# Two tokens of V in a partition row, heads in pairs on halves of the matmul array: one change to an attention and routed-expert kernel

## The chip, the cores and the metric

The kernel runs on one core of one Trainium2 chip. The metric is the device time of one execution in microseconds; the time of the kernel before is the median of three runs, and one further execution was profiled.

## The reference

Attention of 8 batches x 8 heads with head dimension 64: 512 local tokens that attend to a band of 32 tokens on each side and to 32 global tokens, and 32 global tokens that attend to everything. Its output, 8 x 544 rows of 512 numbers, goes through eight experts with a capacity of 80 rows each; a row that no expert keeps comes out as zeros.

```python
s_g = scale * q_g @ k_all.T                    # global queries over all keys
out_g = softmax(s_g) @ v_all
s_ll = where(abs(i - j) <= 32, scale * q_l @ k_l.T, -1e9)
s_lg = scale * q_l @ k_g.T
out_l = softmax(concat(s_lg, s_ll)) @ concat(v_g, v_l)
x = concat(out_g, out_l)                       # (4352, 512)
probs = softmax(x @ w_gate); expert = argmax; gate = its probability
for e in range(8):
    rows = those of e, cut to the 80 of the largest gate
    out[rows] = gate[rows] * (relu(x[rows] @ w1[e]) @ w2[e])
```

## The kernel before

The program is written out in order by hand: what stands first in the source stands first on its engine. A step q is half a batch, four heads; there are 16 steps, and the loop over them (L691 to L819) interleaves the work of steps q to q + 4. An index t or u below counts blocks of 64 or 128 tokens of a head, j = 0, 1 a pair of heads.

- SP issues nearly all loads: `load_qk` (q and k four steps ahead), `load_v` (V two steps ahead, L214, and with every even step the global values vg of the batch, four transfers, L218, into one of two buffers). After them in a step come the stores of x (`Ld`) and some stores of zeros to the output (`zeros`, L638): 17 in all, six in the loop and eleven behind it.
- V lies in `vb` with one token of a head in a partition: 128 partitions, 16 blocks of 64 numbers and a 1 beside them that makes the sum of the weights. The rows that a transfer moves are 256 bytes. `shift_v` (POOL, L224 to L226) makes a second copy shifted by 64 tokens, for the odd blocks.
- `T_chunk` transposes q and k on PE (L299); ACT copies them to SBUF (L307). `kO_copy` and `qw_copy` (POOL) make the wrapped ends and the shifted copy of k.
- `L_fill(q, j)` puts the banded scores of two heads into two PSUM tiles, 16 matmuls of 64 rows by 128 columns (L362), one head on the upper and one on the lower half of the rows; the band of the first head is added by a matmul with `bandneg` (L353), that of the second is multiplied in by POOL after the exponential (`mask`, L375).
- `G_fill` and `Q_fill` make the scores against global keys (L328) and of global queries (L340, five matmuls of 128 x 128 for each j).
- `G_all` (L396) begins the output of all four heads with the global part, `H_chunk(q, h)` (L409) adds the local part of one head: eight products, each as two passes of fp32, 128 rows by 64 columns. After heads 1 and 3, DVE divides by the sum (L416, L417) into `xn`. `Q_chunk` (L432) does the same for the global queries.
- `X_chunk` transposes `xn` for the gate's logits (L447), `C_chunk` (POOL, L458) packs it for the store; `La` to `Ld` make logits, gates and the stores of a batch, spread over the next steps; `some(n)` runs pieces of the list of the best rows on DVE. `warm(n)` are matmuls whose result nobody reads.

In a step the order on PE is: G_all, H(0), Q_chunk, T(q+2), L_fill(q+1, 0), H(1), L_fill(q+1, 1), T(q+2), H(2), H(3), G_fill(q+1), Q_fill, X, Q_fill, X. Expert weights come on POOL's queue, one or two parts of 512 KB a step. Behind the loop stand the choice of rows (DVE), the gathers (L912), the experts and the scatters (L950).

Of the kernel before, what the change touches and what calls it, by code (L numbers as in the profile page):

```python
# [26 lines left out]
def _np_consts(B, S, SG, cap):  # L27
# [5 lines left out]
    p = np.arange(P)[:, None]  # L33
    i = np.arange(64)[None, :]
    band = np.zeros((P, 8, 64), dtype=np.float32)
    for t in range(8):
        w = p if t % 2 == 0 else np.where(p < 64, p + 64, p - 64)
        band[:, t, :] = (w - i >= 0) & (w - i <= 2 * WIN)
    band[:, 7, :] *= (p >= 64) == (i < 32)
# [43 lines left out]
def kernel(  # L83
# [57 lines left out]
    vb = [vpool.tile([P, 32, 65], FP32, name=f"vb{i}") for i in range(3)]  # L141
# [45 lines left out]
    band = cpool.tile([P, 8, 64], FP32, name="band")  # L187
# [12 lines left out]
    def preset_v(i):  # L200
        nc.vector.memset(vb[i][:, 0:16, 64:65], 1.0)
# [4 lines left out]
    vg = [apool.tile([P, 2, 65], FP32, name=f"vg{i}") for i in range(2)]  # L206
    for i in range(2):
        nc.gpsimd.memset(vg[i][:, :, 64:65], 1.0)

    def load_v(q):  # L210
        b, qd = divmod(q, 2)
        hs = slice(4 * qd, 4 * qd + 4)
        v = vb[q % 3]
        nc.sync.dma_start(out=v[:, 0:16, 0:64], in_=v_l[b, hs].rearrange("h (u p) d -> p (h u) d", p=P))  # L214
        if qd == 0:
            for r in range(4):
                h = 2 * (r % 2) + r // 2
                nc.sync.dma_start(out=vg[b % 2][32 * r:32 * r + 32, :, 0:64],  # L218
                                  in_=v_g[b].rearrange("(q f) g d -> f g q d", f=4)[h])

    def shift_v(q):

        v = vb[q % 3][:].rearrange("p (o h u) d -> p o h (u d)", o=2, u=4)
        nc.gpsimd.tensor_copy(out=v[0:64, 1, :, 0:195], in_=v[0:64, 0, :, 65:260])  # L224
        nc.gpsimd.tensor_copy(out=v[0:64, 1, :, 195:260], in_=v[0:64, 0, :, 0:65])
        nc.gpsimd.tensor_copy(out=v[64:128, 1], in_=v[64:128, 0])  # L226

    load_v(0)
    load_qk(1)
# [12 lines left out]
    def load_wg():  # L242
        nc.sync.dma_start(out=wg[:, :, 0:E], in_=moe_w_gate.rearrange("(c p) e -> p c e", p=P))
        for q in range(2):
            nc.sync.dma_start(out=wgq[64 * q:64 * q + 64],
                              in_=moe_w_gate[256 * q:256 * q + 256].rearrange("(h d) e -> d h e", d=64))
# [18 lines left out]
    def setup_globals(b0, b1, *ts):  # L265
        for t, bd in ((1, kbd), (0, qbd)):
# [9 lines left out]
            for x, y, r, f in parts:  # L276
                nc.vector.tensor_copy(out=bd[x, b0:b1, r, 32 * f:32 * f + 32], in_=src[y, :, :, f, :])


    qkT = [apool.tile([P, 2, 1120], FP16, name=f"qkT{i}") for i in range(2)]  # L280
    kO = [apool.tile([P, 2, 4, 2, 64], FP16, name=f"kO{i}") for i in range(2)]
# [14 lines left out]
    def T_chunk(q, t, cp=None):  # L296
        T_ps = psT([P, 8, 2, 64], FP16, f"T_ps{q}_{t}")
        for i in range(8):
            nc.tensor.transpose(out=T_ps[:, i].rearrange("x a p -> x (a p)"),  # L299
                                in_=qkr[q][:, t, i].rearrange("p g d -> p (g d)"), identity=ident16[:, :])  # L300
        dst = qkT[q % 2][:, :, 544 * t:544 * t + 512].rearrange("x a (p i) -> x a p i", i=8)
        src = T_ps[:].rearrange("x i a p -> x a p i")
        if cp:
            for a in range(2):
                cp[a](out=dst[:, a], in_=src[:, a])
        else:
            nc.scalar.copy(out=dst, in_=src)  # L307

    def qw_copy(q):

        (nc.gpsimd if q else nc.vector).tensor_copy(out=qkT[q % 2][:, :, 512:544], in_=qkT[q % 2][:, :, 0:32])

    def kO_copy(q, *aa):

        for a in aa or range(2):
            eng = nc.gpsimd if q or a else nc.vector
            buf = qkT[q % 2][:, a]
            eng.tensor_copy(out=buf[:, 1056:1120], in_=buf[:, 544:608])
            eng.tensor_copy(out=kO[q % 2][:, a],  # L319
                            in_=buf[:, 608:1120].rearrange("x (u w y) -> x u w y", w=2, y=64)[:, :, ::-1, :])  # L320

    def G_fill(q):
# [4 lines left out]
        for j in range(2):  # L327
            nc.tensor.matmul(out=g_ps[64 * j:64 * j + 64, :], lhsT=kbd[:, b, 2 * qd + j, :],  # L328
                             rhs=qkT[q % 2][:, j, 32:544], start=True, stop=True)
        nc.scalar.activation(out=s["eG"][:], in_=g_ps[:], func=AF.Exp, scale=scale)  # L330

    def Q_fill(q, j):
        b, qd = divmod(q, 2)
        gq_ps = psS([P, NB, 64], FP32, f"gq_ps{q}_{j}")
        for u in range(NB):
            if u < 4:
                k = qkT[q % 2][:, j, 544 + 128 * u:672 + 128 * u]
            else:
                k = kbd[:, b, 2 * qd:2 * qd + 2, :].rearrange("x r c -> x (r c)")
            nc.tensor.matmul(out=gq_ps[:, u, :], lhsT=k, rhs=qbd[:, b, 2 * qd + j, :], start=True, stop=True)  # L340
        eQ = hpool.tile([P, NB, 64], FP32, tag="eQ", bufs=4, name=f"eQ{q}_{j}")
        nc.scalar.activation(out=eQ[:], in_=gq_ps[:], func=AF.Exp, scale=scale)
        st[q]["eQ"].append(eQ)

    def L_fill(q, j):

        s = st.setdefault(q, {"eL": {}, "eQ": []})
        buf = qkT[q % 2][:, j]
        l_ps = [psS([P, 512], FP32, f"l_ps{q}_{j}_{hh}") for hh in range(2)]
        under = q >= QB  # L350
        if under:

            nc.tensor.matmul(out=l_ps[0][:], lhsT=ident16[:, :], rhs=bandneg[:].rearrange("p t i -> p (t i)"),  # L353
                             start=True, stop=False, skip_group_check=True)
        for t in range(8):
            for hh in range(2):
                o = 64 * hh
                if t % 2 == 0:
                    lhsT = buf[o:o + 64, 544 + 64 * t:672 + 64 * t]
                else:  # L360
                    lhsT = kO[q % 2][o:o + 64, j, t // 2].rearrange("x w y -> x (w y)")
                nc.tensor.matmul(out=l_ps[hh][:, 64 * t:64 * t + 64], lhsT=lhsT,  # L362
                                 rhs=buf[o:o + 64, 64 * t + 32:64 * t + 96], start=(hh == 1 or not under), stop=True,
                                 skip_group_check=True)
        for hh in range(2):
            eL = hpool.tile([P, 512], FP32, tag="eL", bufs=8, name=f"eL{q}_{j}_{hh}")
            nc.scalar.activation(out=eL[:], in_=l_ps[hh][:], func=AF.Exp, scale=scale)  # L367
            s["eL"][2 * hh + j] = eL

    def mask(q, j):  # L370

        for hh in range(q >= QB, 2):
            eng = nc.gpsimd if q else nc.vector
            eL = st[q]["eL"][2 * hh + j]
            eng.tensor_tensor(out=eL[:], in0=eL[:], in1=band[:].rearrange("p t i -> p (t i)"), op=ALU.mult)  # L375
# [11 lines left out]
    def G_all(q):  # L387
# [3 lines left out]
        s["o2"] = [psO(f"o_ps{q}_{i}")[:, :, 0:260].rearrange("p h (u d) -> p h u d", u=4) for i in range(2)]  # L391
        s["o"] = [s["o2"][h // 2][:, h % 2] for h in range(4)]
        for u in range(4):
            for r in range(4):
                h = 2 * (r % 2) + r // 2
                nc.tensor.matmul(out=s["o"][h][:, u, :],  # L396
                                 lhsT=s["eG"][32 * r:32 * r + 32, 128 * u:128 * u + 128],
                                 rhs=vg[b % 2][32 * r:32 * r + 32, qd, :], start=(u == 0), stop=False,
                                 skip_group_check=True)

    def H_chunk(q, h):
# [3 lines left out]
        o = s["o"][h]  # L405
        for u in range(4):
            for odd in range(2):
                t = 2 * u + odd
                nc.tensor.matmul(out=o[64 * odd:64 * odd + 64, u, :],  # L409
                                 lhsT=s["eL"][h][:, 64 * t:64 * t + 64],  # L410
                                 rhs=v[:, 16 * odd + 4 * h + u, :], start=False, stop=True,
                                 skip_group_check=True)
        if h % 2:
            o2 = s["o2"][h // 2]
            rec = hpool.tile([P, 2, 4], FP32, tag="rec", bufs=4, name="rec")
            nc.vector.reciprocal(out=rec[:], in_=o2[:, :, :, 64])  # L416
            nc.vector.tensor_tensor(  # L417
                out=s["xn"][:, :, 64 * h - 64:64 * h + 64].rearrange("p u (h d) -> p h u d", h=2),
                in0=o2[:, :, :, 0:64], in1=rec[:].unsqueeze(3).to_broadcast([P, 2, 4, 64]), op=ALU.mult)

    def Q_chunk(q):
# [3 lines left out]
        og = psT([P, 65], FP32, f"og{q}")  # L425
        for u in range(NB):
            for h in range(4):
                f = slice(32 * (h // 2), 32 * (h // 2) + 32)
                r = 2 * (h % 2) + h // 2
                x = slice(32 * r, 32 * r + 32)  # L430
                eQ = s["eQ"][h % 2]
# [568 lines left out]
```

## Time and profile before

| | us |
|---|---|
| runs | 272.04, 274.37, 275.7 (median 274.37) |
| profiled execution | 272.33 |
| its span, first to last instruction | 270.6 |
| mean granted clock of TensorE | 0.937 |
| start of the vg matmuls of steps 1, 8, 9, 14, 15 | 25.6, 102.4, 116.3, 168.2, 183.5 |
| start of the first gather | 226.65 |

The span falls into three parts: loads and the first step up to 25.6 us, the loop up to about 191 us, and the choice of rows, gathers and experts. In the page a row names line, engine, operation, result<-inputs, shapes and number, then busy time and mean of one in ns, then the idle time before it and what ended that. "issue" stands for idle time that ended with nothing the profile shows. Matmuls overlap in the array, so PE's busy time isn't the time that the array computes; the distance between starts is the better measure.

The costliest rows of PE and POOL:

```profile
L375 POOL TENSOR_TENSOR eL<-eL,band 128x512 f32<-128x512 f32 x30 | 38.6, 1285 | 21.9 <-ACT eL L367 21.7
...
L409 PE MATMUL o_ps<-vb,eL 128*64 128x65 f32 x1024 | 43.9, 231 | 0.4 <-issue 0.3
...
L224 POOL COPY vb<-vb 64x780 f32<-64x780 f32 x16 | 13.9, 868 | 7.6 <-DMA vb<-in_v_l_dram 7.6
...
L226 POOL COPY vb<-vb 64x1040 f32<-64x1040 f32 x16 | 17.0, 1064 | 0.9
```

### The profile page before, as it was taken

Reading aid. Unit: us, or ns where it says so; the run is one execution under the profiler, and the core shown is the slowest. Engines: PE = TensorE matmul, PEld = TensorE weight load, DVE = VectorE, ACT = ScalarE, POOL = GpSimd, SP = SyncE. Lnnn points to the kernel's source line nnn. Section 1 sums busy time; section 2 is a strip of 40 time slices with the busy share of each in tenths; the row PEclk is TensorE's granted clock in tenths of the full one; section 3 lists DMA queues with packets and bytes.
Section 4 is the critical chain, followed back from the end, with each engine's and each line's share of the span. In section 5 each row is a group of like instructions: output and inputs, shape, how many; then the busy total and the mean of one; then the engine's idle time right before and its main releaser. Section 6 shows DMA issues by size and latency. Waiting matters only on the chain.

```text
span 270.6 us, 9574 instructions
## 1 busy us (share of the span) xinstructions
PE 234.3 (87%) x4031; PEld 160.4 (59%) x4031; DVE 151.7 (56%) x447; ACT 134.7 (50%) x236; POOL 165.2 (61%) x260
## 2 busy tenths in 40 slices
PE   6888898999899958989999999979939999479990
PEld 2467666776686747667677676557414435357750
DVE  2657534636743763478477689286878972002210
ACT  4657569679569580859669668240130000023430
POOL 2539987698697808777887898674540004752231
PEclk9799999999999996899999999795997999959997
DMA  7999899977989699899999899998999999289811
GB/s 226 253 305 221 276 249 239 289 165 156 299 255 205 226 216 277 152 240 310 174 275 262 174 207 167 268 208 159 162 205 223 233 417 417 91 161 212 208 48 48
DMA packets 67739, 60.05 MB, mean 222 GB/s; under 512 B 46192, under 2 KB 50544, under 8 KB 67696
## 3 DMA queue, kind: packets, MB, share of 16 engines
q1 hardware_dynamic: 59712, 40.61, 52.3%
q0 software_dynamic: 7840, 18.80, 39.1%
q8 instruction: 31, 0.51, 0.8%
q14 instruction: 12, 0.10, 0.1%
q10 hardware_dynamic: 144, 0.03, 0.1%
HBM read 61.57 MB, written 14.70 MB: 282 GB/s over the span
## 4 chain that ended last, share of the span: by engine, by line
PE 40%; DMA 19%; issue 12%; POOL 10%; DVE 5%; SPq 5%; ACT 5%; POOLq 1%; ACTq 0%; DVEq 0%
PE o_ps L409 9%; DMA vg<-in_v_g_dram 6%; PE o_ps L396 5%; DMA x_scr<-xgb 5%; PE og L432 5%; PE T_ps L299 4%; PE x_ps L447 3%; PE lt_ps L472 3%; DMA x_scr<-xb 3%; PE l_ps L362 3%; ACT qkT L307 3%; POOL out_dram L950 2%; DMA out_dram<-zt 2%; SPq L218 2%; PE l_ps L353 2%
## 5 line engine op out<-in xcount | busy, mean ns | idle before, releaser
L375 POOL TENSOR_TENSOR eL<-eL,band 128x512 f32<-128x512 f32 x30 | 38.6, 1285 | 21.9 <-ACT eL L367 21.7
L307 ACT COPY qkT<-T_ps 128x1024 f16<-128x1024 f16 x31 | 31.5, 1017 | 36.1 <-PE T_ps L299 35.9
L409 PE MATMUL o_ps<-vb,eL 128*64 128x65 f32 x1024 | 43.9, 231 | 0.4 <-issue 0.3
L409 PEld LDWEIGHTS o_ps<-vb,eL 128*64 128x64 f32 x1024 | 35.7, 141 | 11.7 <-issue 7.7
L367 ACT ACTIVATE eL<-l_ps 128x512 f32<-128x512 f32 x64 | 35.1, 606 | 12.6 <-PE l_ps L362 12.5
L165 ACT CAST qkr<-qkb 128x1024 f16<-128x1024 f32 (+1 forms) x26 | 26.9, 1040 | 3.8 <-DMA qkb<-in_q_l_dram 3.5
L651 PE MATMUL w_ps<-w1sb,onesb 128*128 128x512 bf16 x121 | 28.7, 391 | 0.0
L936 ACT ACTIVATE fhT<-h_ps 128x320 bf16<-128x320 f32 x16 | 6.5, 431 | 40.9 <-remote 39.3
L912 POOL DMA_INDIRECT xg<-x_scr,idx x8 | 7.8, 974 | 28.7 <-DMA out_dram<-zt 26.5
L396 PE MATMUL o_ps<-vg,eG 32*128 32x65 f32 x512 | 20.8, 291 | 3.8 <-DMA vg<-in_v_g_dram 3.8
L447 PE MATMUL x_ps<-misc,xn 128*128 128x128 f32 x128 | 21.0, 288 | 3.4 <-DVE xn L417 2.6
L417 DVE TENSOR_TENSOR xn<-o_ps,rec 128x512 f32<-128x512 f32 x32 | 22.1, 692 | 2.5 <-DVE rec L416 0.5
L416 DVE RECIPROCAL rec<-o_ps 128x8 f32<-128x8 f32 x32 | 6.6, 206 | 29.9 <-PE o_ps L409 29.9
L396 PEld LDWEIGHTS o_ps<-vg,eG 32*128 32x128 f32 x512 | 18.3, 199 | 6.6 <-DMA vg<-in_v_g_dram 4.3
L299 PE MATMUL T_ps<-ident,qkr 128*128 128x128 f16 x256 | 20.3, 223 | 1.8 <-ACT qkr L165 1.2
L458 POOL CAST xb<-xn 128x1024 bf16<-128x1024 f32 x16 | 16.6, 1039 | 6.7 <-DVE xn L417 6.7
L651 PEld LDWEIGHTS <-onesb 128*128 128x128 bf16 x121 | 11.6, 100 | 14.9 <-issue 2.9
L319 POOL COPY kO<-qkT 128x512 f16<-128x512 f16 x31 | 19.0, 614 | 1.9
L224 POOL COPY vb<-vb 64x780 f32<-64x780 f32 x16 | 13.9, 868 | 7.6 <-DMA vb<-in_v_l_dram 7.6
L950 POOL DMA_INDIRECT out_dram<-y,idx x8 | 7.4, 928 | 17.9 <-ACT y L948 17.3
L299 PEld LDWEIGHTS <-qkr 128*128 128x128 f16 x256 | 15.2, 99 | 4.6 <-ACT qkr L165 1.9
L226 POOL COPY vb<-vb 64x1040 f32<-64x1040 f32 x16 | 17.0, 1064 | 0.9
(156 smaller groups left out, 474.0 us busy)
## 6 DMA issues: line engine op xcount, KB each, us to landing
out_dram<-zt SPq DMA_DIRECT2D x17, 512.0 KB, 7.0
qkb<-in_q_l_dram SPq DMA_DIRECT2D x16, 512.0 KB, 5.4
qkb<-in_k_l_dram SPq DMA_DIRECT2D x16, 512.0 KB, 6.7
vb<-in_v_l_dram SPq DMA_DIRECT2D x16, 512.0 KB, 9.1
w2sb<-in_moe_w_dram POOLq DMA_DIRECT2D x12, 512.0 KB
w1sb<-in_moe_w_dram POOLq DMA_DIRECT2D x10, 512.0 KB
x_scr<-xb SPq DMA_DIRECT2D x8, 385.5 KB, 9.7
vb<-in_moe_w_dram POOLq DMA_DIRECT2D x6, 512.0 KB
```

The lines of the kernel that those rows point to most:

```text
L165: cp(out=qkr[q][:, t, i].rearrange("p i g d -> p g i d"), in_=qkb[q % 2][:, t, :, i])
L226: nc.gpsimd.tensor_copy(out=v[64:128, 1], in_=v[64:128, 0])
L299: nc.tensor.transpose(out=T_ps[:, i].rearrange("x a p -> x (a p)"), in_=qkr[q][:, t, i].rearrange("p g d -> p (g d)"), identity=ident16[:, :])
L307: nc.scalar.copy(out=dst, in_=src)
L319: eng.tensor_copy(out=kO[q % 2][:, a], in_=buf[:, 608:1120].rearrange("x (u w y) -> x u w y", w=2, y=64)[:, :, ::-1, :])
L367: nc.scalar.activation(out=eL[:], in_=l_ps[hh][:], func=AF.Exp, scale=scale)
L375: eng.tensor_tensor(out=eL[:], in0=eL[:], in1=band[:].rearrange("p t i -> p (t i)"), op=ALU.mult)
L396: nc.tensor.matmul(out=s["o"][h][:, u, :], lhsT=s["eG"][32 * r:32 * r + 32, 128 * u:128 * u + 128], rhs=vg[b % 2][32 * r:32 * r + 32, qd, ...
L409: nc.tensor.matmul(out=o[64 * odd:64 * odd + 64, u, :], lhsT=s["eL"][h][:, 64 * t:64 * t + 64], rhs=v[:, 16 * odd + 4 * h + u, :], start=F ...
L417: nc.vector.tensor_tensor(out=s["xn"][:, :, 64 * h - 64:64 * h + 64].rearrange("p u (h d) -> p h u d", h=2), in0=o2[:, :, :, 0:64], in1=re ...
L447: nc.tensor.transpose(out=x_ps[:, 128 * u:128 * u + 128], in_=s["xn"][:, u, 128 * j:128 * j + 128], identity=identf[:, :])
L651: nc.tensor.matmul(out=w_ps[:], lhsT=onesb[:], rhs=w1sb[0][:, 0, 0:512], start=True, stop=True)
```

## The change

V is laid out with two neighbouring tokens of a head in a partition row: 64 partitions hold 128 tokens, heads 0 and 1 of a step lie on partitions 0 to 63, heads 2 and 3 on 64 to 127, and the rows that a transfer moves are 512 bytes. The scores are made by the parity w of the key: keys of one parity and 64 rows of one head on one quarter of the array, so each product of `L_fill`, `H_chunk`, `Q_chunk` and `Q_fill` is cut in two, and what used 128 rows now uses 64. The two PSUM tiles of `L_fill` are now the two parities. Even tokens have a 1 in column 0 and odd tokens one in column 129, so the sum of the weights stands in two columns, which DVE adds up first. H has two calls a step, each with a pair of heads, and the first stands behind the next step's scores. The global values have three buffers and their transfers are issued at the head of an even step, ahead of q, k and V. One store of zeros moves from the loop to behind it (loop steps 3, 8, 10, 12, 13); `Lm` of step 14 stands behind H, and five `warm` matmuls are added there.

```diff
-    vb = [vpool.tile([P, 32, 65], FP32, name=f"vb{i}") for i in range(3)]
+    vb = [vpool.tile([P, 2, 8, 130], FP32, name=f"vb{i}") for i in range(3)]
...
-    band = cpool.tile([P, 8, 64], FP32, name="band")
+    band = cpool.tile([P, 2, 8, 64], FP32, name="band")
...
-    vg = [apool.tile([P, 2, 65], FP32, name=f"vg{i}") for i in range(2)]
+    vg = [apool.tile([P, 2, 66], FP32, name=f"vg{i}") for i in range(3)]
...
-        nc.sync.dma_start(out=v[:, 0:16, 0:64], in_=v_l[b, hs].rearrange("h (u p) d -> p (h u) d", p=P))
-        if qd == 0:
-            for r in range(4):
-                h = 2 * (r % 2) + r // 2
-                nc.sync.dma_start(out=vg[b % 2][32 * r:32 * r + 32, :, 0:64],
-                                  in_=v_g[b].rearrange("(q f) g d -> f g q d", f=4)[h])
+        for g in range(2):
+            nc.sync.dma_start(out=v[64 * g:64 * g + 64, 0, :, 1:129],
+                              in_=v_l[b, hs][2 * g:2 * g + 2].rearrange("h (s p w) d -> p (h s) (w d)", s=4, w=2))
+
+    def load_vg(b):
+        for r in range(4):
+            nc.sync.dma_start(out=vg[b % 3][32 * r:32 * r + 32, :, 1:65],
+                              in_=v_g[b].rearrange("(q f) g d -> f g q d", f=4)[r])
...
-        nc.gpsimd.tensor_copy(out=v[0:64, 1, :, 0:195], in_=v[0:64, 0, :, 65:260])
-        nc.gpsimd.tensor_copy(out=v[0:64, 1, :, 195:260], in_=v[0:64, 0, :, 0:65])
-        nc.gpsimd.tensor_copy(out=v[64:128, 1], in_=v[64:128, 0])
+        nc.gpsimd.tensor_copy(out=v[:, 1], in_=v[:, 0])
+        for x in (slice(0, 32), slice(64, 96)):
+            e, o = (v[x, i].rearrange("p (g s) d -> p g (s d)", g=2) for i in range(2))
+            nc.gpsimd.tensor_copy(out=o[:, :, 0:390], in_=e[:, :, 130:520])
+            nc.gpsimd.tensor_copy(out=o[:, :, 390:520], in_=e[:, :, 0:130])
...
-    qkT = [apool.tile([P, 2, 1120], FP16, name=f"qkT{i}") for i in range(2)]
-    kO = [apool.tile([P, 2, 4, 2, 64], FP16, name=f"kO{i}") for i in range(2)]
+    qT = [apool.tile([P, 2, 544], FP16, name=f"qT{i}") for i in range(2)]
+    kT = [apool.tile([P, 2, 2, 256], FP16, name=f"kT{i}") for i in range(2)]
+    kO = [apool.tile([P, 2, 2, 4, 2, 32], FP16, name=f"kO{i}") for i in range(2)]
...
+            eng.tensor_copy(out=o[:, :, :, 1], in_=e[:, :, :, 1])
+            eng.tensor_copy(out=o[:, :, 0:3, 0], in_=e[:, :, 1:4, 0])
+            eng.tensor_copy(out=o[:, :, 3, 0], in_=e[:, :, 0, 0])
...
+            for f in range(2):
+                x, o = slice(64 * f, 64 * f + 64), 64 * f + 32 * j
+                nc.tensor.matmul(out=g_ps[o:o + 32, :], lhsT=kbd[x, b, 2 * qd + f, 32 * j:32 * j + 32],
+                                 rhs=qT[q % 2][x, j, 32:544], start=True, stop=True, skip_group_check=True)
...
+        for u in range(8):
+            for f in range(2):
+                x = slice(64 * f, 64 * f + 64)
+                nc.tensor.matmul(out=gq_ps[x, 32 * u:32 * u + 32],
+                                 lhsT=kT[q % 2][x, j, u // 4, 64 * (u % 4):64 * (u % 4) + 64],
+                                 rhs=qbd[x, b, 2 * qd + j, 32 * f:32 * f + 32], start=True, stop=True,
+                                 skip_group_check=True)
+        nc.tensor.matmul(out=gq_ps[:, 256:320], lhsT=kbd[:, b, 2 * qd:2 * qd + 2, :].rearrange("x r c -> x (r c)"),
+                         rhs=qbd[:, b, 2 * qd + j, :], start=True, stop=True, skip_group_check=True)
...
         for t in range(8):
-            for hh in range(2):
+            for k in range(4):
+                f, w = k % 2, (k + k // 2) % 2
+                x = slice(64 * f, 64 * f + 64)
...
+                nc.tensor.matmul(out=l_ps[w][x, 64 * t:64 * t + 64], lhsT=lhsT,
+                                 rhs=qT[q % 2][x, j, 64 * t + 32:64 * t + 96], start=(w == 1), stop=True,
                                  skip_group_check=True)
...
-    def H_chunk(q, h):
+    def H_chunk(q, j):
...
+            for w in range(2):
+                for odd in range(2):
+                    t = 2 * u + odd
+                    for f in range(2):
+                        x = slice(64 * f, 64 * f + 64)
+                        nc.tensor.matmul(out=s["o"][j + 2 * f][64 * odd:64 * odd + 64, u, w:w + 65],
+                                         lhsT=s["eL"][j, w][x, 64 * t:64 * t + 64],
+                                         rhs=v[x, odd, 4 * j + u, 65 * w:65 * w + 65], start=False, stop=True,
+                                         skip_group_check=True)
+        den = hpool.tile([P, 2, 4], FP32, tag="den2", bufs=4, name="den2")
+        nc.vector.tensor_reduce(out=den[:], in_=o2[:, :, :, 0:66:65], axis=AX.X, op=ALU.add)
...
+        for u in range(8):
+            w, i = divmod(u, 4)
             for h in range(4):
...
+                nc.tensor.matmul(out=og[32 * h:32 * h + 32, w:w + 65], lhsT=s["eQ"][j][x, 32 * u:32 * u + 32],
+                                 rhs=v[x, 0, 4 * j + i, 65 * w:65 * w + 65], start=False, stop=(u == 7),
+                                 skip_group_check=True)
...
+        if qd == 0 and 0 < q and b + 1 < B:
+            load_vg(b + 1)
         if 0 < q and q + 4 < NQ:
             load_qk(q + 4)
...
         G_all(q)
-        H_chunk(q, 0)
         Q_chunk(q)
...
-        H_chunk(q, 1)
+        H_chunk(q, 0)
...
-            if q == NQ - 2:
-                Lm(pend)
...
-        H_chunk(q, 2)
...
-        H_chunk(q, 3)
+        H_chunk(q, 1)
         if q == NQ - 2:
+            Lm(pend)
             Lb2(pend)
...
             Lb3(pend)
+            warm(5)
...
-        if q in (3, 4, 5, 8, 12, 13):
+        if q in (3, 8, 10, 12, 13):
             zeros(1)
```

The gate's weights come in four transfers instead of one to match the new order of heads, `C_chunk` permutes as it packs, and the copies of q for step 1 go from POOL to DVE.

## The prediction

> **What bounds the kernel now.** First the page's table of engines, then the busy time by stage over fourteen whole steps of the loop (from the vg matmuls of step 1 at 25.6 us to those of step 15, the last, at 183.5):
>
> ```profile
> PE 234.3 (87%) x4031; PEld 160.4 (59%) x4031; DVE 151.7 (56%) x447; ACT 134.7 (50%) x236; POOL 165.2 (61%) x260
> ...
> 25.60:183.50 157.90, 144.76 (x3040) 106.44 (x3040) 97.09 (x284) 106.38 (x179) 123.81 (x195) 0.96 0.97 228
> ```
>
> Columns of the second line: window, length, busy PE, PEld, DVE, ACT, POOL, granted clock, DMA share, GB/s. A step lasts 157.9/14 = 11.3 us; PE is busy for 92% of it, the DMA engines for 97%, POOL for 78%. PE sets the pace; the DMA engines decide how often it stalls. So next the waits of PE and PEld between 25 and 190 us (total, times, longest):
>
> ```profile
> PE o_ps L396 <- DMA vg<-in_v_g_dram: 3.8, 2, 3.1
> PE x_ps L447 <- DVE xn L417: 2.1, 2, 1.9
> PE og L432 <- issue: 2.1, 3, 1.2
> ...
> PEld o_ps L409 <- issue: 7.7, 10, 1.4
> ```
>
> The late vg costs PE some 4.3 us and a second time through the clock: after the 3.3 us wait at 99 us the window 102.4 to 116 has clock 0.75, and a stretch that takes 3.5 us elsewhere (vg matmuls to the next scores) takes 6.2. With the waits at 169 and 180 us I put the slow-clock loss at 4.7 us, and the wait for xn at 2.4.
>
> The "issue" rows need the timeline, here PE around 120 us:
>
> ```profile
> 118.49 0.31 PE L432 MATMUL og<-vg,eQ 32*32 32x65 f32 x6
> 120.03 0.27 PE L432 MATMUL og<-vg,eQ 32*32 32x65 f32 x2 [1.23 <-issue]
> ```
>
> PE stops in the middle of a row of eight equal matmuls and nothing is named. In the trace's list of LDWEIGHTS and MATMUL eight such gaps (0.31 to 1.45 us, together 5.6) lie whole multiples of 254 to 255 instructions apart. That is the spacing of the page's instruction queue:
>
> ```profile
> q8 instruction: 31, 0.51, 0.8%
> ```
>
> 31 packets of 16 KB are 0.51 MB[...]. So PE's program arrives in pages of some 255 instructions. By the trace's packets, for 24 pages of the loop: a page's packet starts some time after PE entered the page before (in us: 0.5 0.7 0.9 1.3 1.3 1.6 1.7 1.9 2.4 2.5 2.5 2.8 3.1 3.1 3.3 3.5 3.7 3.8 3.9 4.3 4.5 5.1 5.3 6.0; mean 2.9), takes 1.1 us, and at a stall PE goes on about 0.65 us after it landed. It stalls exactly when this sum, mean 4.65 us, exceeds the time in which PE uses a page up: now 6.4 us.
>
> [...] Trace: 128x64 tiles (L409) start in pairs every 58 ns, 128x32 (L432) in fours every 56, 64x128 (L362) in pairs every 29; a change costs 0.1 to 0.15 us. [...] In the window 47.0 to 47.6 us all 547 packets are V's 256 B ones, at 137% of 16 engines: 24 ns each. [...]
>
> **The change, part by part** (a step is half a batch).
> *Scores* (L362): 32 matmuls of 64x128 become 64 of 64x64, only the two diagonal quarters used. Still pairs in 29 ns: 0.46 to 0.93 us, +0.46.
> *Weighted V* (L409): 64 passes in pairs, 64 x 29 = 1.86 us, become 128 in quarters; if four run at once, 128 x 14.5 = 1.86. Fewer changes of mode: -0.15. Bounds: -0.3, and +1.86 if only two run at once; L432's fours speak for the first.
> *Global queries over V* (L432): 32 passes become 64, fours in 56 ns: +0.45.
> *Q_fill* (L340): 10 matmuls of 33 ns become 32 half as wide plus two. No row has a 64x64 f16 load; L328 (128x64, 109 ns against L340's 97 for 128 columns) says a narrow load isn't cheaper. I take 15 ns each and two mode changes per fill: +0.45; bounds 0 and +0.8. *G_fill, G_all*: same columns, 0.
> PE in sum: **+1.2 us a step**, bounds +0.6 and +3.
> *PE's program*: +2 x (32 scores + 64 V + 32 queries + 24 Q_fill + 2) = +308 instructions a step; 3040/14 = 217 matmuls, each with its load, a step now, 371 then; the window's fourteen steps pass through 41 pages, not 24.
> *V by DMA*: 2048 packets of 256 B become 1024 of 512 B. Between 24 ns (no dearer) and 48; I take 32, on the line to the 2 KB packets (some 81 ns in the window 69.0 to 70.4): 49 - 33 = 16 us of one engine, 1.0 us of the sixteen, of some 10.9 a step (0.97 x 11.3). One more issue on SP, 0.43 us.
> *vg*: four issues (0.43 each) move ahead of q, k and V. SP stood 10.3 us at those four at 64.9 us, behind V's packets; q and k come 1.7 us later at most, and are needed a step or more on. The third vg buffer takes away the wait for the last reader; G_all and the global queries of two steps later are the first to need it. Late next is V itself, for POOL's shift; H now stands behind the next scores, 2 to 3 us later, which covers that.
> *POOL*: shift 868 + 416 + 1064 ns becomes 1064 + 2 x (868 + 416), taking rows of 64 partitions for 32: +1.28 (bounds +0.4, +1.3); kO's copies 1.7 to 1.3. Net +0.9 on 123.8/14 = 8.85: 9.75 of a step, hidden by PE's 11.3 below; mask and kO wait behind the shift, and their readers come half a step later.
> *Order of H*: H(0) moves behind the queries, a transpose and the next scores; what stands behind it on PE stays the same, and its result is needed at X(0) at the end of the step, 4 us later. xn(0) still frees its PSUM tile before the next step's G_all asks for it. Cost 0; the cover is that distance, and if it were gone DVE's 1.1 us would show.
> *DVE*: 48 reductions at 0.19 (row of L521): 9 us beside PE. Between H(1) and X(1) they add 0.2, covered by G_fill, both Q_fill and X(0), 1.4 us.
> *ACT, C_chunk, preset, qw and kbd layouts*: same elements, 0; their cover is that ACT ends no wait of PE above 0.8 us.
> *Prologue*: bandneg 128 KB larger, three more issues for wg, four for the vg of batch 1: +0.5. *Lm moved behind H, five warm matmuls* (1.1 us in a gap of 1.9): the xn wait shrinks; counted in what is saved. *Zeros*: five issued in the loop, not six; twelve remain in the tail at 1.06 us an issue, and the gathers begin at 226.65 us, when a zero transfer lands: +1.
>
> **The sum.** Without today's stalls (4.3 + 4.7 + 2.4 + 5.0 inside the window) a step is (157.9 - 16.4)/14 = 10.1 us; with +1.2, 11.3; times 14/40.8, a page is used up in 3.88 us, less than the 4.65 it takes to come. Putting the 24 waits of today in turn, each page taking the longer of 3.88 and wait + 1.75, the mean is 4.95: 202 us, +44. But the waits depend on the DMA engines: the shortest (0.5 and 0.9 us, at 27 and 89 us) fall where they were nearly idle, the long ones under V or weights. V's packets fall by a third and a longer loop spreads the rest: load 0.97 to about 0.8. Waits at 0.7 give 4.25: 173 us, **+16**; at 0.5, 162, +4. I take 0.7. With 0.5 + 1 from above and 1 for step 15: 270.6 + 18.5 = 289; with the 1.7 us that the profiled execution (272.33) has around its span, **291**. That execution lies 0.7% below the median of the runs shown, 274.37, and the forecast is not shifted for it.
>
> **Rivals.** (A) *The program page is the bound*, as above: 280 to 319 (waits at 0.6 to 1). Against it: the waits may fall more. (B) *Only PE's work counts*, pages come in time: waits at 0.5 or less, 0 to +4 in the window, with the rest 275 to 279. (C) *Faster*: the load on the DMA engines is the real bound, 97%, and V's relief pays: all four stalls go and PE's work grows by only 0.6. 14 x 10.7 = 150, -8, with +2.5: 267. It decides when quarters overlap better than the pairs in L362 show and Q_fill is free; against it, PE waits for DMA in 4.3 us of 158 only. (D) *POOL becomes the bound*: at +1.3 and with its waits for ACT (20 us in the loop) it takes 8.85 + 1.3 + 1.4 = 11.6 a step; above 11.3 it decides: 162, +4, and as it makes PE wait too, some 280. (E) *The quarters don't run four at once*: +1.9 a step, 185 us, +27: 302. That the early vg is late all the same would add 7 to any of these.
>
> **Numbers.** A 0.48, B 0.22, C 0.17, D 0.08, E 0.05. A measurement of this kernel can tell about 2%, 5.5 us. Against 274.37 the bounds are 268.9 and 279.9. C gives faster, 0.15; B is mostly within, with the edges of C and D: 0.25; A, E and the rest slower, 0.6. The range from 267 (half of C left out) to 313 (A with waits at 0.9) leaves out some 0.2. The slower cases alone span 280 to 313.
>
> **What would show it.** Some 51 packets on the instruction queue; "issue" gaps on PE some 255 instructions apart, at more than half the pages instead of a third, in sum over 15 us; no wait for vg; clock 0.75 gone from 102 us; L362's successor in pairs every 29 ns, L409's in fours every 58; POOL 78 to 85% of a step; DMA share about 0.8. I am wrong if the pages land well ahead of their use, or if H's starts come in pairs.

## The result, and the profile after

| | before | after |
|---|---|---|
| median of the runs side by side, us | 275.03 (272.04 to 276.67, 4 runs) | 336.46 (335.07 to 340.29, 4 runs) |
| ratio | 1 | 1.226, 95% interval 1.212 to 1.240 |
| span of the profiled execution, us | 270.6 | 334.2 |
| fourteen whole steps of the loop, us | 157.9 | 213.4 |

Ratios here and below compare the fast runs alone (a run more than 1.5% above the fastest of its kernel counts as slow), medians take all runs, so a ratio need not be that of the medians beside it.

The changed kernel is slower by 61 us; forecast were 291 us, and a range from 267 to 313. Of the 63.6 us between the two spans, 55.5 lie in the fourteen whole steps (vg matmuls of step 1 to those of step 15), 7.3 ahead of them, 0.8 behind them. Of the 7.3, one stall of PE in step 0 makes 4.7: it lies just 256 instructions behind another one, so it belongs to the kind described below.

The page of the kernel after, its tables of engines and of DMA queues:

```profile
PE 274.4 (82%) x6500; PEld 199.4 (60%) x6500; DVE 154.7 (46%) x497; ACT 137.9 (41%) x236; POOL 179.3 (54%) x281
...
q8 instruction: 51, 0.84, 1.1%
```

PE runs 6500 matmuls where it ran 4031, and 51 pages of program arrive instead of 31; with a weight load to each matmul that is 13000 instructions, 255 to a page, where it was 8062, 260 to a page. Every engine is busy for a smaller share than before: nothing that computes has become the bound. The busy time by stage, for the fourteen steps and then for one of them (window, length, busy PE, PEld, DVE, ACT, POOL, granted clock, DMA share, GB/s):

```profile
32.90:246.30 213.40, 178.84 (x5201) 140.28 (x5201) 98.45 (x326) 108.86 (x179) 134.75 (x208) 0.87 0.73 165
...
217.20:232.00 14.80, 14.11 (x367) 11.27 (x366) 8.32 (x33) 6.82 (x13) 7.83 (x15) 0.65 0.69 140
```

The granted clock fell from 0.96 to 0.87 over the loop, and to 0.65 in that step: PE's busy time grew by 34 us, part of it at half speed. PE is idle for 34.6 us of the window, where it was idle for 13.1. What it waits for, by the waits of PE in that window (total, times, longest):

```profile
PE o_ps L440 <- issue: 12.2, 7, 2.4
PE l_ps L394 <- issue: 9.7, 4, 4.3
PE o_ps L427 <- issue: 3.2, 2, 2.0
PE og L468 <- issue: 3.0, 2, 2.3
PE gq_ps L369 <- issue: 1.9, 1, 1.9
```

(L440 is now H, L394 the scores, L427 the vg matmuls, L468 the global queries, L369 Q_fill.) No row names vg or V, none names an engine with more than 1.9 us, and nearly all of it is "issue". The timeline of PE shows what such a wait looks like:

```profile
69.03 0.23 PE L394 MATMUL l_ps<-qT,kT 64*64 64x64 f16 x4
69.09 0.22 PE L394 MATMUL l_ps<-qT,kO 64*64 64x64 f16 x3
73.58 0.19 PE L394 MATMUL l_ps<-qT,kO 64*64 64x64 f16 x1 [4.27 <-issue]
...
74.38 1.91 PE L440 MATMUL o_ps<-vb,eL 64*64 64x65 f32 x60
```

PE stops after three of four equal matmuls, for 4.27 us. Then it runs at half clock: 60 of the 64 passes of H take 1.91 us here, and all 64 take 1.16 us at full clock elsewhere in this trace (at 144.16 us, for one). In the list of starts of PE's LDWEIGHTS and MATMUL there are 21 gaps over 0.3 us in the window that lie whole multiples of 255.6 instructions apart, together 36.0 us. In the kernel before there were nine, 5.6 us.

I count three things below in this way for each kernel, for the window from step 1 to step 15. **Page gaps**: starts of PE instructions over 0.3 us apart, within four instructions of such a multiple. (Gaps of 0.31 to 0.57 us also recur in every step for other reasons, and a few of these fall on a multiple by chance: 1.5 of the 36.0 us in the kernel after, and probably most of the 2.4 in the kernel before without loads.) **Half clock**: time of the window in which the trace grants 0.5. **DMA share**: as the profile has it.

### The profile page after: what moved, and what is told of

It reads as the page before. It is cut to its first block, busy times and chain, and to the rows that moved or that the text cites. A ratio compares the mean times of both kernels' runs of the same rounds, so it can differ in the third digit from the quotient of the medians.

```text
span 334.2 us, 14602 instructions
## 1 busy us (share of the span) xinstructions
PE 274.4 (82%) x6500; PEld 199.4 (60%) x6500; DVE 154.7 (46%) x497; ACT 137.9 (41%) x236; POOL 179.3 (54%) x281
## 4 chain that ended last, share of the span: by engine, by line
PE 60%; issue 17%; DMA 8%; DVE 4%; POOL 4%; ACT 2%; SPq 1%; POOLq 1%; DVEq 0%; ACTq 0%
PE o_ps L440 13%; PE l_ps L394 7%; PE og L468 6%; PE T_ps L324 6%; PE o_ps L427 6%; PE x_ps L485 5%; DMA x_scr<-xgb 4%; PE gq_ps L369 3%; PE l_ps L384 3%; PE lt_ps L512 3%; DMA out_dram<-zt 2%; POOL out_dram L990 2%; PE G_ps L358 2%; PE lg L522 1%; PE og L461 1%
## 5 line engine op out<-in xcount | busy, mean ns | idle before, releaser
L406 POOL TENSOR_TENSOR eL<-eL,band 128x512 f32<-128x512 f32 x30 | 38.1, 1269 | 68.4 <-ACT eL L399 66.2
L440 PE MATMUL o_ps<-vb,eL 64*64 64x65 f32 x2048 | 46.6, 244 | 16.7 <-issue 16.7
L440 PEld LDWEIGHTS o_ps<-vb,eL 64*64 64x64 f32 x2048 | 40.7, 155 | 26.0 <-issue 24.7
L331 ACT COPY qT<-T_ps 128x1024 f16<-128x1024 f16 x16 | 16.2, 1012 | 45.6 <-PE T_ps L324 45.6
L394 PE MATMUL l_ps<-qT,kO 64*64 64x64 f16 x512 | 21.9, 201 | 9.7 <-issue 9.7
L232 POOL COPY vb<-vb 32x780 f32<-32x780 f32 x32 | 27.3, 854 | 1.7
L468 PE MATMUL og<-vb,eQ 64*32 64x65 f32 x1024 | 23.8, 253 | 3.5 <-issue 3.5
L394 PEld LDWEIGHTS <-kT 64*64 64x64 f16 x512 | 18.2, 115 | 13.2 <-issue 12.5
L427 PE MATMUL o_ps<-vg,eG 32*128 32x66 f32 x512 | 22.1, 311 | 3.2 <-issue 3.2
L468 PEld LDWEIGHTS og<-vb,eQ 64*32 64x32 f32 x1024 | 20.2, 129 | 6.1 <-issue 5.1
L427 PEld LDWEIGHTS o_ps<-vg,eG 32*128 32x128 f32 x512 | 19.4, 217 | 6.4 <-issue 5.8
L394 PE MATMUL l_ps<-qT,kT 64*64 64x64 f16 x512 | 22.4, 203 | 0.0
```

The lines of the kernel that those rows point to most:

```text
L232: nc.gpsimd.tensor_copy(out=o[:, :, 0:390], in_=e[:, :, 130:520])
L394: nc.tensor.matmul(out=l_ps[w][x, 64 * t:64 * t + 64], lhsT=lhsT, rhs=qT[q % 2][x, j, 64 * t + 32:64 * t + 96], start=(w == 1), stop=True, ...
L406: eng.tensor_tensor(out=eL[:], in0=eL[:], in1=band[:, 1].rearrange("p t i -> p (t i)"), op=ALU.mult)
L427: nc.tensor.matmul(out=s["o"][h][:, u, :], lhsT=s["eG"][x, 128 * u:128 * u + 128], rhs=vg[b % 3][x, qd, :], start=(u == 0), stop=False, sk ...
L440: nc.tensor.matmul(out=s["o"][j + 2 * f][64 * odd:64 * odd + 64, u, w:w + 65], lhsT=s["eL"][j, w][x, 64 * t:64 * t + 64], rhs=v[x, odd, 4 ...
L468: nc.tensor.matmul(out=og[32 * h:32 * h + 32, w:w + 65], lhsT=s["eQ"][j][x, 32 * u:32 * u + 32], rhs=v[x, 0, 4 * j + i, 65 * w:65 * w + 65 ...
```

## The experiments

The theory: PE's program arrives in pages of some 255 instructions; 308 more a step make a page last less long than the next one takes to come; and behind a stall of some 2 us the clock is mostly halved for a while (3.4 to 10.2 us in the trace of the kernel after). The rivals: the array itself (quarters, changes of mode, longer sums), or the fetch as such whatever the DMA engines carry.

| kernel | pages | window, us | page gaps, us | half clock, us | DMA share |
|---|---|---|---|---|---|
| before | 31 | 157.9 | 5.6 | 11.9 | 0.97 |
| before + early vg alone | 31 | 162.4 | 4.9 | 18.9 | 0.94 |
| before + 12 large matmuls a step | 33 | 163.7 | 5.6 | 3.4 | 0.95 |
| before + 77 tiny ones a step | 41 | 182.7 | 16.8 | 35.4 | 0.84 |
| before + 154 tiny ones a step | 51 | 219.4 | 42.7 | 71.7 | 0.69 |
| before, loads left out | 31 | 144.6 | 2.4 | 0 | 0.32 |
| after | 51 | 213.4 | 36.0 | 55.9 | 0.73 |
| after, late vg | 51 | 211.9 | 36.8 | 58.0 | 0.74 |
| after, q and k left out | 51 | 200.0 | 30.0 | 32.8 | 0.57 |
| after, V left out | 51 | 193.6 | 29.3 | 21.8 | 0.60 |
| after, loads left out | 51 | 170.9 | 10.6 | 6.8 | 0.26 |

Each row is one profiled execution, and they come from several chips: the median of the kernel before was 264.8 to 275.0 us in the sets that they belong to. So a difference of a few us between two rows says nothing.

**Instructions with little array work.** The kernel before gets the change's number of PE instructions, and nothing else of it.

```diff
+    def extra(q, n):
+        for i in range(n):
+            x = slice(32 * (i % 4), 32 * (i % 4) + 32)
+            nc.tensor.matmul(out=st[q]["ob"][x, 1, 300:301], lhsT=ident16[x, x], rhs=ident16[x, 0:1],
+                             start=False, stop=True, skip_group_check=True)
...
         G_all(q)
+        extra(q, 26)
```

(ob is one of o's two PSUM tiles; the other five calls stand at the four H_chunk and behind Q_chunk.)

> The kernel before with 154 tiny matmuls more in each step (32x32 weights, one column, into an unused column of o's PSUM tile), which is the 308 PE instructions a step that the change adds, and almost no array work. Theory (pages of program): about 50 packets of program, gaps of 1 to 4 us some 255 instructions apart as in the kernel after, granted clock of the loop below 0.92: 305 to 335 us. Rival (the change is slow because of the array: quarters, mode changes, longer sums): 154 x 7 to 14 ns is 1 to 2 us a step, so 285 to 300 us, with the issue gaps near the 5.6 us of the kernel before.

Measured: 343.89 us against 273.25 for the kernel before on the same chip, ratio 1.272 (1.253 to 1.291). One line of its window, then its waits of PE:

```profile
30.90:250.30 219.40, 182.80 (x5196) 141.39 (x5200) 91.16 (x285) 107.77 (x179) 122.58 (x192) 0.84 0.69 161
```

```profile
PE o_ps L390 <- issue: 17.5, 10, 3.5
PE o_ps L417 <- issue: 7.5, 5, 2.7
PE T_ps L299 <- issue: 5.1, 2, 4.5
```

L390 is the tiny matmul. The added instructions make the kernel before as slow as the change does, slower by 9 us than I expected at most. They aren't free on the array: at full clock a call of 26 takes 0.26 us, so 154 take some 1.5 us a step, 21 us in fourteen steps (an estimate from this trace). That is within the 1 to 2 us a step that the rival allowed. The window grew by 61.5 us, and it has the change's two marks, 42.7 us of page gaps and a clock of 0.84, which the rival doesn't explain.

**Array work with few instructions.** The control: 12 large matmuls a step, in the same tile.

```diff
+            nc.tensor.matmul(out=st[q]["ob"][:, 1, 300:492], lhsT=ident16[:, :],
+                             rhs=bandneg[:, 0:3, :].rearrange("p t i -> p (t i)"), start=False, stop=True,
+                             skip_group_check=True)
...
         G_all(q)
+        extra(q, 4)
```

> The control to it: the kernel before with 12 large matmuls more in each step (128x128 weights, 192 columns of f16 into unused columns of o's PSUM tile, in three groups of four): 12 x 0.08 us and three mode changes are 1.2 us of array work a step as in the change, but only 24 instructions. Theory (pages of program): a page lasts as long as before or longer, issue gaps at most the 5.6 us of before: 282 to 296 us. Rival (array work sets the time of the change): as long as the kernel with the tiny ones, or longer.

Measured: 277.88 us against 273.25, ratio 1.025 (1.008 to 1.043).

```profile
26.70:190.40 163.70, 155.67 (x3206) 114.98 (x3204) 98.07 (x285) 106.77 (x179) 122.56 (x193) 0.99 0.95 220
```

The profiled execution took 281.21 us, the longest of the four. The starts of the large matmuls lie some 0.086 us apart, about the 0.08 us expected (an estimate from the page's row of them: 24.5 us of busy time for 48 groups of four, 0.251 us for one). PE is busy for 10.9 us more in its window than in the kernel before, and the window is 5.8 us longer: no wait for vg is left in it, and the half clock is 3.4 us instead of 11.9. The median lies 4 us below the theory's interval, probably for that reason. So array work of a like amount costs 2.5% (0.8 to 4.3) with 24 instructions a step, and 27.2% with 308. The array rival falls.

**Half the dose.** The tiny matmuls at 13 instead of 26 a call.

> The kernel before with half as many tiny matmuls, 77 a step, 154 PE instructions. Theory (a page is used up faster than the next one comes): a page then lasts (10.1 + 0.5) x 14 / 32.5 = 4.6 us, close to the mean arrival of 4.65: some 41 packets of program, gaps of 10 to 25 us in the window and half clock after the longer ones, 285 to 310 us. Rival (cost in proportion to the tiny matmuls, 70 us for 154): 308 us or more.

Measured: 298.75 us, in the theory's interval. But on that chip the median of the kernel before was 266.08 us: the first 77 cost 32.7 us, and 154 cost 70.6 on the other chip. That is close to proportion, so the time doesn't decide between theory and rival, which had been set against 273 us. The page gaps speak for the theory: they grow by 11.2 us for the first 77 and by 25.9 for the next.

**One part alone: vg early.** The kernel before with three vg buffers, loaded at the head of even steps.

```diff
+        if qd == 0 and 0 < q and b + 1 < B:
+            load_vg(b + 1)
         if 0 < q and q + 4 < NQ:
             load_qk(q + 4)
```

> The kernel before with one part of the change alone: global values loaded at the head of every even step, ahead of that step's other loads, in three buffers. Theory (PE's program arrives in pages, and every stall of some 2 us also halves the clock for a while): PE has no more instructions than before, so only the removed waits count: the two vg waits of 3.8 us go, and most of the half clock after them: 264 to 270 us, 24 to 31 packets of program. Rival (the early loads push q, k and V back and their readers wait instead): 273 to 279 us with waits for V or qkr in place of those for vg.

Measured: 275.13 us against 273.25, ratio 1.015 (1.001 to 1.029). No gain, and the rival's side. No wait names vg any more; this one, from its waits of PE in the window, has come instead (besides 3.1 us for V, in two waits):

```profile
PE G_ps L330 <- ACT eL L369: 6.1, 1, 6.1
```

ACT's timeline at that place says why:

```profile
93.45 0.60 ACT L369 ACTIVATE eL<-l_ps 128x512 f32<-128x512 f32 x1
101.08 1.04 ACT L165 CAST qkr<-qkb 128x1024 f16<-128x1024 f32 x1 [7.03 <-DMA qkb<-in_q_l_dram]
102.03 1.08 ACT L369 ACTIVATE eL<-l_ps 128x512 f32<-128x512 f32 x2
```

ACT sits in the regrouping of q for 7.03 us, because q's transfer is late, and the exponentials that PE needs next are queued behind it. With the DMA engines at 0.94 of the loop, the early load of vg was paid for by a later one of q.

**The part undone in the kernel after.** vg behind V again, two buffers.

```diff
-        if qd == 0 and 0 < q and b + 1 < B:
-            load_vg(b + 1)
...
             load_v(q + 2)
+            if qd == 0:
+                load_vg(b + 1)
```

> The kernel after with one part undone: global values loaded behind V again, into two buffers. Theory (the early load is worth nothing while the page of program decides): 334 to 340 us, and no wait for vg over 1 us, since the slower loop leaves the loads time. Rival (the early load is worth its 4 to 8 us): 340 to 346 us with vg waits of 3 us.

Measured: 333.81 us, on a chip on which the kernel before took 266.08: ratio 1.265 (1.251 to 1.280), beside the change's 1.226 (1.212 to 1.240). As ratios, that would make the late vg slower by 3%. But these are different chips, so both kernels were put side by side on one.

> The kernel after once more, on the same chip as the next, since the runs with the late vg had a chip on which the kernel before took 266 us, not 275. Both theories: 1.20 to 1.25 times the kernel before.

> The kernel after with global values loaded behind V again, into two buffers, beside the kernel after on one chip. Theory (the early load is worth nothing while pages of program decide): within 1.5% of the kernel after. Rival (early values are worth 4 to 8 us): 1.5 to 2.5% longer than the kernel after.

Measured: medians of 339.96 us for the kernel after, 340.28 with the late vg, 271.21 for the kernel before (1.25 times, the end of what I expected). The lowest of each, 333.22, 331.30 and 268.30 us, give 1.24 times and a late vg that costs nothing. So in the kernel after the early load isn't worth the rival's 1.5% either. The kernel before itself moves by 4% between sets of runs, so a part worth 1 to 3% can only be judged side by side.

**What the pages wait for.** First the expert weights: 11 of the 12 loads of the resident experts go behind step 15.

```diff
-    WS = [0, 0, 1, 2, 3, 4, 5, 6, 7, 8, 9, 10, 12] + [12] * 4
+    WS = [0, 0] + [1] * 14 + [12]
```

> The kernel after with 11 of its 12 loads of resident expert weights issued behind step 15 instead of one a step; PE's program is unchanged. The experts at the end wait for them, so only the loop counts: from step 1's vg matmuls to step 12's, 170.6 us in the kernel after (122.1 before). Theory (pages arrive late because of what lies in the DMA engines ahead of them): page waits above 2 us become few, the sum of the issue gaps falls by half or more, 135 to 152 us in that window. Rival (array work, or the fetch itself, whatever the DMA load): 165 to 171 us.

Measured: 163.3 us in that window from step 1 to step 12, where the kernel after takes 170.6. A miss for the theory as I put it: the page gaps there fell from 32.9 to 23.2 us, not by half, and the half clock rose from 44 to 51 us. So weights are at most one load among several. Then everything at once: weights late, and q, k and V not loaded in the loop.

```diff
-        if 0 < q and q + 4 < NQ:
-            load_qk(q + 4)
-        if not first and q + 2 < NQ:
-            load_v(q + 2)
```

> The kernel after, left out: the loads of q and k from the sixth half batch on and of V from the fourth on (old values stay in the buffers); 11 of the 12 resident expert loads stand behind step 15. PE's program is unchanged. Only the loop counts, from step 1's vg matmuls to step 15's: 213.4 us in the kernel after. Theory (a page's packet waits behind what lies in the DMA engines): page waits of 0.1 to 1.2 us as they are today where the DMA engines are idle, issue gaps under 5 us in sum instead of 36, no half clock from them: 158 to 172 us, about 14 x (10.1 + 1.2) = 158. Rival (the fetch itself cannot keep this pace): gaps stay, over 190 us.

> The same loads left out of the kernel before, whose loop takes 157.9 us from step 1 to step 15. Theory: PE's own work is left, 14 x 10.1 = 141 to 150 us, so the change's array work is the difference to the kernel after without these loads, predicted as 1.2 us a step or 17 us. Rival (the array work of the change was priced far too low, quarters not four at once): the difference is over 30 us.

The windows, of the kernel after without these loads, and of the kernel before without them (where the transfers of vg stand in `load_v` and are left out too):

```profile
33.40:204.30 170.90, 157.50 (x5201) 122.96 (x5205) 103.80 (x327) 107.52 (x179) 127.04 (x196) 0.98 0.26 62
```

```profile
24.70:169.30 144.60, 136.60 (x3037) 101.59 (x3036) 98.57 (x285) 105.94 (x179) 116.44 (x182) 1.00 0.32 79
```

The same program of 5201 matmuls, with the DMA engines at 0.26 instead of 0.73, takes 42.5 us less, and has its clock back. Page gaps are left with 10.6 us rather than under 5; 3.4 of these lie behind step 12, where the weights of a later expert are still loaded. The page packets of that window start on average 1.2 us after PE entered the page before, 32 of 40 at 1.24 us or less; in the kernel after the average is 2.3. So the fetch alone keeps the pace well enough. The difference between the two windows, 26.3 us, leaves 16.3 for the array work of the change when the page gaps (10.6 and 2.4) and 1.8 us for the half clock (an estimate from the spacing of starts) are taken off. That is 1.16 us a step.

Last, q and k alone and V alone are left out. Both ran on a chip on which the kernel before took 264.81 us, so some of what the windows gain may be the chip.

> The kernel after, left out: the loads of q and k from the sixth half batch on; V and the expert weights are loaded as before. From step 1's to step 15's vg matmuls: 213.4 us in the kernel after, 170.9 with neither q, k, V nor 11 expert loads in the loop. Theory (the long page waits stand under the 2 KB packets of q and k and under the weights, not under V): with q and k gone the page gaps fall from 36 to some 15 us and the half clock with them, 178 to 192 us. Rival (V's packets set the waits, as the prediction had it when it scaled them by V's relief): above 200 us.

> The kernel after, left out: the loads of V from the fourth half batch on; q, k and the weights are loaded as before. Theory (V is the smaller part of the waits): page gaps 20 to 32 us, window 192 to 208 us. Rival (V's packets set the waits): gaps under 15 us, below 190 us; and if the relief of V does nothing at all for the waits, 210 us or more.

The windows, without q and k, then without V:

```profile
31.70:231.70 200.00, 169.61 (x5201) 132.31 (x5205) 98.48 (x327) 108.38 (x179) 134.77 (x209) 0.92 0.57 119
```

```profile
32.00:225.60 193.60, 165.13 (x5202) 129.06 (x5201) 100.99 (x326) 108.31 (x179) 134.43 (x208) 0.94 0.60 147
```

The first misses the theory's interval by 8 us and lies at the edge of the rival's, the second lies in the theory's. Each takes 6 to 7 us off the page gaps, as the weights took 10 off in the shorter window; all together took 25. No one load holds the pages up: in the kernel after the gaps go with the sum of what the DMA engines carry, 36.0 us at a DMA share of 0.73, 30.0 and 29.3 at 0.57 and 0.60, 10.6 at 0.26. In the kernel after the 47 page packets that can be read so start 0.09 to 4.5 us after PE entered the page before, and not evenly: 26 of them later than 2 us. Inside the window, 13 of the 16 that started within 1.21 us had the DMA engines under 15% busy in about the microsecond before; 19 of the 20 that started at 2.5 us or later had them at 84% or more.

That the half clock hangs on the gaps is read from the trace, not from a run of its own: each of the twelve stretches at half clock in the kernel after's window begins within 2.2 us of the end of a gap of 1.49 us or more (page gaps but one). Three gaps of 1.84 to 2.48 us in it have no such stretch. Without the loads there is one stretch, behind a gap of 2.68 us; the seven gaps from 1.09 to 1.43 us in that window have none. No length of gap divides the two in all traces: in the kernel before a stretch begins 1.8 us behind a gap of 0.96 us, and without the loads it has a gap of 2.56 us and no stretch.

## Why the prediction was right in direction and wrong in size

**What held.** Pages of program: 51 packets as forecast. Issue gaps 255 apart, over 15 us in sum, at half of the pages. Array work: 1.2 us a step forecast, 1.16 measured; scores start in pairs every 29 ns, passes of H in fours every 58 ns, 14.4 ns for one, so rival E falls. POOL: 9.75 us a step forecast, 134.75/14 = 9.63 measured, and no wait on it; rival D falls. (As a share of the longer step that is 63%, not 78 to 85.) No wait for vg. The moved H, the reductions on DVE (175 ns each), Lm and the warm matmuls show in no wait above 2 us. Tail +0.8 us, forecast with +1 for step 15 and +1 for the zeros.

**What failed: the terms of the late pages and of the half clock behind them.** The sum had +16 us in the window: +16.8 of array work, -16.4 for the stalls of before, and +15.6 for pages that come late. Measured, by the trace's gaps and clock:

| term | forecast, us | measured, us |
|---|---|---|
| array work | +16.8 | +16.3 |
| stalls of before that go: late pages 5.6, other gaps 6.9, half clock 3.7 | -16.4 | -16.2 |
| page gaps | +15.6 | +36.0 |
| half clock after them | 0 | +16.6 |
| sum | +16 | +52.7, of +55.5 |

The half clock's 16.6 us: 2249 PE instructions of the window start at half clock, on average 23.8 ns apart, 16.4 ns at full clock (gaps cut at 0.6 us). 2.8 us of the window are not accounted for.

Three steps of the prediction are behind this.

*"V's packets fall by a third ... Waits at 0.7."* V's 512 B packets took 44.5 ns in the loop, not 32; the 256 B ones of before took 21.1. So the transfers of V cost as much as before, twice the time for half the packets, and the relief of 1.0 us a step was none: the DMA engines work 0.73 x 213.4 = 156 us in the window, where they worked 0.97 x 157.9 = 153. The share fell only because the loop got longer. I had taken this price from a line between two other packet sizes; the bound I named and didn't take, 48 ns, was nearer. The size alone doesn't set the price: with q and k left out, V's packets took 38.1 ns on average, and half of them 27 or less. The mean of the page waits did fall, to 2.3 us, 0.8 of the 2.9 of before, but by idle stretches between bursts, and a mean hides that half of the waits are still 2 to 4.5 us long. The working's own formula with these waits, one by one, gives some 30 us of page gaps where 15.6 were forecast.

*"At a stall PE goes on about 0.65 us after it landed."* The traces don't show this. At 120.03 us, the stall that the prediction shows, the page's packet had ended at 118.55, 1.48 us earlier. At the six page gaps of the kernel before above 0.45 us PE's next instruction starts 1.38 to 1.48 us after the end of the packet; at the 17 of the kernel after above 0.6 us, 1.25 to 1.59, 1.42 on average. So each late page was priced some 0.8 us too short. Put right, the formula gives some 34 us at the prediction's 0.7, close to the 36.0, and 48 with the waits that were measured. That is too much: it lets PE use up every page in 3.88 us, and at half clock a page takes longer (6.28 us from 185.23 us on), so that the next one comes in time. How the 20 us divide between the waits and this term stays open.

*A new stall was priced at its length.* For the stalls of before I counted the half clock behind them as a second cost, 4.7 us. For the stalls that the change adds I counted none. That is 16.6 of the 37 us by which the sum came out short; the page gaps are the other 20.

Two steps more failed. *"Prologue: ... +0.5"*: the sum had no late page there, and 7.3 us were measured, 4.7 of them the stall in step 0. And *"Late next is V itself"*, which didn't show in the time: the kernel before with the early vg alone shows q late next, through ACT, with 6.1 us against 3.1 for V; the wait removed was worth nothing.

Rivals B and C had the pages coming in time; the 21 page gaps of the kernel after rule them out. C's ground was not empty: without loads the kernel before runs its window in 144.6 us instead of 157.9. But the change doesn't relieve the DMA engines.

No version tried beats the kernel before. Not tried: loads cut smaller and spread over the step, so that the DMA engines are less often at 84% or more when a page is due. Open: what a burst of given size costs a page's packet. Open too: whether the price of V's packets has to do with where they land, rows of 520 B that start 4 B late.

## What to carry to other kernels

Count PE's instructions before splitting matmuls, not just the array's time: here a page of some 255 instructions (weight load and matmul each count) had to last about 5 us while the DMA engines were busy, since its packet started 2.3 to 2.9 us on average after PE entered the page before, took 1.1 us, and PE went on 1.4 us after that. In the kernel after PE used up the pages without a stall at full clock in 3.7 to 4.3 us, and half of the pages ended in a stall. Price a stall of PE of some 2 us twice, once for its length and once for the half clock that mostly follows. And price a new packet size from both neighbours, taking the end that gains nothing (here 48 ns; 44.5 were measured) unless a trace shows it.

## What the runs showed of the hardware

- 154 matmuls of one column a step lengthened fourteen steps by 61.5 us, 37.1 of them in page gaps. With the DMA engines at about 0.7 (the kernel after and the one with these matmuls) the page gaps came to 36 to 43 us, and with them at 0.26 (the kernel after without the loads) to 10.6.
- At the end of a stall PE's next instruction started 1.2 to 1.6 us after the page's packet had ended, in both kernels.
- V at 512 B a packet moved no faster than at 256 B: 44.5 against 21.1 ns a packet, with 102 ns for the 2 KB of q and k in the kernel after. With q and k left out the packets of 512 B took 38.1 ns.
- In the kernel after, gaps of PE of 1.49 to 4.46 us were mostly followed by 3.4 to 10.2 us of half clock, and three gaps of 1.84 to 2.48 us were not.
